# One transfer for q and k of a head, the projection loaded into its place, eight constant products in hash attention with a gated feed-forward block

## The chip, the cores and the metric

The kernel runs on one core of a Trainium2 chip. The metric is device time in microseconds (us). Engines are named as the profile names them: PE is the matrix engine (TensorE; PEld is its loading of weights), DVE the vector engine, ACT the scalar engine, POOL GpSimd, SP the engine that here only issues transfers. SP, ACT and POOL each have a queue of their own in which they issue DMAs.

## The reference

Attention over 4 batches x 8 heads, 768 positions of 64 numbers, in which a query sees only the keys in its own hash bucket; the result goes through a feed-forward block of 3072 tokens x 512, with 2048 inner columns.

```python
q_bits = (np.einsum('bhsd,dk->bhsk', q, proj) > 0).astype(np.int64)
k_bits = (np.einsum('bhsd,dk->bhsk', k, proj) > 0).astype(np.int64)
powers = 2 ** np.arange(n_bits)
q_bucket = np.sum(q_bits * powers, axis=-1)
k_bucket = np.sum(k_bits * powers, axis=-1)
mask = q_bucket[:, :, :, None] == k_bucket[:, :, None, :]
scores = np.where(mask, scale * np.matmul(q, k.transpose(0, 1, 3, 2)), -1000000000.0)
...
attn = attn / (np.sum(attn, axis=-1, keepdims=True) + 1e-09)
...
h = x @ w_in
sp = np.maximum(h, 0.0) + np.log1p(np.exp(-np.abs(h)))
g = h * erf(sp)
return (g @ w_out).astype(np.float32)
```

There are six bits, so `proj` is 64 x 6. q, k, v and `proj` are float32.

## The kernel before

The host transposes q and k and puts them below one another: `qkT` has, for each of 32 heads, 128 rows, 64 of q and 64 of k, of 768 positions each. `proj2` is 128 x 12: `proj` in the upper left and again in the lower right corner, zeros elsewhere. `bucket` is the column 0 to 63, twice.

Attention works on 16 pairs of heads. A pair's q is a tile of 128 partitions (head a in the first 64, head b in the other 64) by 768, k likewise; v has a tile of the same size. They come from a pool in which each of the three names has three buffers (lines 356 to 360 of `fetch`). A pair takes four kinds of work on PE: the hash products (`bits`), the scores (`st`, in float32, plus products of the bits in bf16 that add a large number where buckets agree), the weighted sum of v (`av`), and a product with ones for the divisors (`z`). ACT takes signs of the bits (L400 for pair 0, L865 later) and exponentials (L595). DVE spreads the sign bits (L411, L421) and adds up the exponentials. Later pairs' bits are put in place with DMAs from POOL (L885, L894). Meanwhile POOL loads the weights of the feed-forward block, which ACT and DVE convert. The feed-forward block follows, with PE lines L1256 and L1374.

The beginning is written out by hand. Pair 0 is loaded in halves of 384 positions (`quick`): q of both heads from SP, k of both heads from ACT's queue for the first half, then the second half from SP, eight transfers in all. Meanwhile PE runs `WARM` = 10 products of a tile of ones (L817) whose result nobody reads. Then, for each half, come the hash products (L387), which need the half's q and k and the tile `proj_sb`, and ACT's sign and DVE's spreading; between the halves stand two sets of scores (`plain`). `proj_sb` is 128 x 64: zeros, but for the projection of head a in rows 0 to 63, columns 0 to 5, and that of head b in rows 64 to 127, columns 32 to 37. To build it, POOL loads `proj2` into `proj_in` (L256), DVE clears `proj_sb` (L257) and copies the two blocks (L260). DVE makes a second, narrower arrangement, `proj_q` (L292), for pairs 1 and on. POOL's second transfer brings `row` (L265); from it DVE makes the constants `steps`, `weight` and `weight_q` (L279 to L298).

The order of all else in attention is set by the planner `arrange`: every step is given an engine, a cost, a rank and what it must follow, and the planner lists them. `start_pair` (L808), which calls `fetch` and `fetch_v` for a pair, is a step of SP with a given cost, and is the same step whatever transfers it holds. For pair 1 and on, q and k are four transfers of 64 x 768, and v is two. ACT's `measure` (L671) reads each q and k once more, for a bound on the scores.

In the last pair, the exponentials of the last two blocks of keys (`NS - 2` and `NS - 1`) go into tiles of the load pool, which has nothing more to load: `block` (L580) takes a q, a k and a v tile for each of the two.

Of the kernel before, what the change touches and what calls it, by code (L numbers as in the profile page):

```python
# [54 lines left out]
F32 = mybir.dt.float32  # L55
# [8 lines left out]
P = 128  # L64
# [133 lines left out]
def kernel(  # L198
# [11 lines left out]
    nc = tc.nc  # L210
    B, H, S, D = v.shape
    NBIT = proj2.shape[1] // 2
# [3 lines left out]
    NC = S // P  # L216
# [13 lines left out]
    const = ctx.enter_context(tc.tile_pool(name="const", bufs=1))  # L230
# [2 lines left out]
    small = ctx.enter_context(tc.tile_pool(name="small", bufs=3))  # L233
    QR = 32
    QB = QR // 2
    WARM = 10
    proj_sb = const.tile([P, 2 * QR], F32, name="proj_sb")
    weight = const.tile([P, 2], F32, name="weight")
    proj_q = const.tile([P, QR], F32, name="proj_q")
# [12 lines left out]
    blocks = []  # L252
    stats = const.tile([P, 2, NPAIR, 2], F32, name="stats")
    nc.vector.memset(ones, 1.0)
    proj_in = const.tile([P, 2 * NBIT], F32, name="proj_in")
    nc.gpsimd.dma_start(out=proj_in, in_=proj2)  # L256
    nc.vector.memset(proj_sb, 0.0)  # L257
    for ab in range(2):
        rows = slice(ab * D, ab * D + D)
        nc.vector.tensor_copy(  # L260
            out=proj_sb[rows, ab * QR : ab * QR + NBIT],
            in_=proj_in[rows, ab * NBIT : (ab + 1) * NBIT],
        )
    row = const.tile([P, 1], F32, name="row")
    nc.gpsimd.dma_start(out=row, in_=bucket)  # L265
    steps = const.tile([P, 8], F32, name="steps")
    for c, (end, factor) in enumerate(
# [12 lines left out]
            out=steps[:, c : c + 1],  # L280
# [9 lines left out]
    for ab in range(2):  # L290
        rows = slice(ab * D, ab * D + D)
        nc.vector.tensor_copy(  # L292
            out=proj_q[rows, ab * QB : ab * QB + NBIT],
            in_=proj_in[rows, ab * NBIT : (ab + 1) * NBIT],
        )
    nc.vector.reduce_sum(out=weight_q, in_=steps[:, 5:8], axis=AX.X)
    nc.vector.tensor_tensor(out=weight_q, in0=weight_q, in1=weight[:, 0:1], op=ALU.add)
# [8 lines left out]
    def bank(name):  # L306
        if "X" in kept:
            return kept["X"]
        return misc.tile([P, 512], F32, name=name, tag="bank")
# [43 lines left out]


    def fetch(i, load, quick=False, early=False, into=None):
        d = into or dict(
            q=load.tile([P, S], F32, name="q", tag="q"),
            k=load.tile([P, S], F32, name="k", tag="k"),
            v=load.tile([P, NC, P], F32, name="v", tag="v"),
        )  # L360
        parts = ((0, "q"), (0, "k"), (1, "k"), (1, "q")) if quick else ((None, "q"), (None, "k"))
        for half, what in parts:
            cols = slice(0, S) if half is None else slice(half * HS, half * HS + HS)
            queue = nc.scalar if quick and what == "k" and half == 0 else nc.sync
            for ab in range(2):
                queue.dma_start(
                    out=d[what][ab * D : ab * D + D, cols],
                    in_=qkT[2 * i + ab, "qk".index(what) * D : "qk".index(what) * D + D, cols],
                )
        if not quick and not early:  # L370
            fetch_v(i, d)
        return d

    def fetch_v(i, d):
        b, j = divmod(i, JP)
        for ab in range(2):
            nc.sync.dma_start(
                out=d["v"][:, :, ab * D : ab * D + D],
                in_=v[b, 2 * j + ab].rearrange("(c p) d -> p c d", p=P),
            )  # L380
# [49 lines left out]
    def attention():  # L430
        NS = NPAIR * 4
        with (
# [21 lines left out]
            e_last = {}  # L454
# [125 lines left out]
            def block(n, c):  # L580
                if n == NS - 2 or n == NS - 1:
                    what, m = "qkv"[c], n - (NS - 2)
                    if (m, c) not in e_last:
                        shape = [P, NC, P] if what == "v" else [P, S]
                        room = load.tile(shape, F32, name=what, tag=what)
                        if what == "v":
                            room = room.rearrange("p c d -> p (c d)")
                        e_last[m, c] = room[:, 0:S].rearrange("p (a c) -> p a c", a=2)
                    return e_last[m, c]
                return (e_odd if n // 2 % 2 else e_even)[:, n % 2 * GC + c, :, :]  # L590

            def exponential(n, c):
                st = pairs[n // 4].pop(("st", n, c))
                e = block(n, c)
                nc.scalar.activation(  # L595
                    out=e[:, :, 0:HS], in_=st[:, :, 0:HS], func=AF.Exp, scale=scale
                )
# [21 lines left out]
            def sum_keys(i, k):  # L619
                d = pairs[i]  # L620
                s = wide_sums[i % 2]
                d["sum"] = s[:, :, 0, :, :] if i < NPAIR - 1 else last_sums
                what, _ = sum_steps(i)[k]
                if what is None:
                    into, one, two = s[:, :, 0, :, :], s[:, :, 0, :, :], s[:, :, 1, :, :]
                elif i == NPAIR - 1 and what[0]:
                    k = what[1]
                    into = last_sums[:, 1, :, :]
                    one = into if k > 1 else block(NS - 2, 0)
                    two = block(NS - 2 + k // GC, k % GC)  # L630
                else:
                    half, first, count = what
                    e = (e_odd if half else e_even)[:, :, :, 0:HS]
                    into = one = s[:, half, :, :, :]
                    if count == 4:
                        one, two = e[:, 0:2, :, :], e[:, 2:4, :, :]
                    elif count == 2:
                        two = e[:, 4:6, :, :]
                    else:
                        into, one, two = last_sums[:, 0, :, :], s[:, 0, 0, :, :], s[:, 0, 1, :, :]  # L640
                nc.vector.tensor_tensor(out=into, in0=one, in1=two, op=ALU.add)  # L641
# [166 lines left out]
            def start_pair(i):  # L808
                pairs[i] = fetch(i, load, early=i == 1)
                if i == 1:  # L810
                    for n in range(2):
                        fetch_v(n, pairs[n])

            pairs[0] = fetch(0, load, quick=True)
            warm = bank("warm")
            for n in range(WARM):
                nc.tensor.matmul(  # L817
                    out=warm[0:D, 0:P],
# [102 lines left out]
            for what, n in order:  # L921
                free = slots[-3] if len(slots) >= 3 else ()
                if what == "score":
                    i = n // 4
# [57 lines left out]
            for h in range(NH):  # L982
                i = h // 2
# [3 lines left out]
            for i in range(NPAIR):  # L987
                n = 4 * i
# [108 lines left out]
    def general(pools):  # L1097
# [16 lines left out]
        if True:  # L1114
            for i in range(NPAIR):
                fetch(i, None, into=d)
                b, j = divmod(i, JP)
                for half in range(2):
# [758 lines left out]
```

## Time and profile before

| what | us |
|---|---|
| median of 3 runs | 900.72 |
| lowest and highest of them | 900.38, 900.77 |
| the profiled execution | 900.89 |
| its span in the profile | 899.1 |

The span is what the profile's clock covers; the profiled execution's own time is 1.79 us longer. Times in the profile count from the span's start. Of the transfers concerned, in the DMA view: 30 of 192 KB each for q and as many for k, issued from SP; for pair 0, four of 96 KB for q and two for k from SP, and two for k from ACT. A median of 4.0 us passes from issue to landing for the 192 KB ones of q, 4.4 for those of k; the projection's 6 KB took 2.7 us, the 0.5 KB of `row` 3.0 us. In the profile "x19" behind an operation is how many instructions a line stands for; PE carries out a float32 product in two instructions that the profile counts, and a few records can be missing.

### The profile page before, as it was taken

To read this page: it belongs to the slowest core of one execution; us is meant where nothing else is said; L and a number is where in the kernel's file an instruction comes from. 1 tells how busy PE (TensorE), PEld (TensorE's weight loads), DVE (VectorE), ACT (ScalarE), POOL (GpSimd) and SP (SyncE) were. 2 spreads that over 40 slices of the span, in tenths; PEclk is the share of its full clock that TensorE was granted. 3 is DMA by queue.
4 is the path that set the end of the run, shared out by engine and by line. 5 is a ranking of instruction groups with operands and counts; after the bars stand their busy time and mean duration, and the time that the engine had idled before them with its cause. 6 is when DMAs were issued, how large, how long until landed. Compare 5 with 4: busy or idle time off the path is not lost.

```text
span 899.1 us, 12500 instructions
## 1 busy us (share of the span) xinstructions
PE 893.8 (99%) x4888; PEld 664.5 (74%) x4888; DVE 667.4 (74%) x836; ACT 577.5 (64%) x808; POOL 58.2 (6%) x97
## 2 busy tenths in 40 slices
PE   9999999999999999999999999999999999999998
PEld 5544444454544588888888888888888888888886
DVE  5999999999999879996566556656776656655653
ACT  6888888788887668855555455555655555545520
POOL 1111211111110000000000001000100000000000
PEclk9999999999999999999999999999999999999999
DMA  9557665676652321201231014211421123001321
GB/s 227 135 161 190 191 161 142 174 199 191 169 145 61 102 89 65 82 35 71 59 98 57 23 47 106 82 36 47 103 84 36 36 59 94 35 19 49 87 72 49
DMA packets 65203, 86.95 MB, mean 97 GB/s; under 512 B 34430, under 2 KB 47790, under 8 KB 65136
## 3 DMA queue, kind: packets, MB, share of 16 engines
q1 hardware_dynamic: 56464, 63.81, 25.0%
q0 software_dynamic: 8224, 21.80, 8.7%
q8 instruction: 40, 0.66, 0.3%
q10 hardware_dynamic: 448, 0.46, 0.2%
q14 instruction: 27, 0.22, 0.1%
HBM read 64.71 MB, written 17.40 MB: 91 GB/s over the span
## 4 chain that ended last, share of the span: by engine, by line
PE 99%; ACT 0%; DVE 0%; issue 0%
PE M L1374 32%; PE X L1256 29%; PE st L568 17%; PE av L653 14%; PE M L1256 4%; PE bits L856 1%; PE bits L697 1%; PE warm L817 0%; PE X L1374 0%; PE bits L387 0%; PE z_ps L697 0%; PE X L697 0%; ACT e_even L595 0%; ACT both L400 0%; DVE u L1411 0%
## 5 line engine op out<-in xcount | busy, mean ns | idle before, releaser
L1296 DVE SCALAR_TENSOR_TENSOR e<-w,e 128x1024 f32<-128x1024 f32 x144 | 173.7, 1221 | 8.4 <-ACT w L1290 3.3
L1256 PE MATMUL X<-area,w_in_sb 128*128 128x256 f32 x680 | 160.6, 379 | 0.0
L1290 ACT ACTIVATE w<-h,cq 128x1024 f32<-128x1024 f32 x144 | 155.5, 1137 | 0.0
L568 PE MATMUL st<-q,k 64*128 64x384 f32 x768 | 155.2, 483 | 0.0
L1278 DVE TENSOR_TENSOR h<-X,h 128x512 f32<-128x512 f32 x65 | 44.8, 689 | 144.7 <-PE X L1256 144.7
L1256 PEld LDWEIGHTS X<-area,w_in_sb 128*128 128x128 f32 x680 | 129.2, 190 | 17.6
L1374 PE MATMUL M<-w_out_sb,h 128*128 128x256 f32 x576 | 141.5, 379 | 0.0
L1256 PE MATMUL X<-area 128*128 128x256 f32 x520 | 122.8, 379 | 0.0
L1274 ACT COPY h<-X 128x512 f32<-128x512 f32 x85 | 49.4, 581 | 112.7 <-PE X L1256 112.5
L1374 PEld LDWEIGHTS M<-w_out_sb,h 128*128 128x128 f32 x576 | 109.4, 190 | 14.9
L1256 PEld LDWEIGHTS X<-area 128*128 128x128 f32 x520 | 98.8, 190 | 13.4
L1286 ACT ACTIVATE e<-h,cq 128x1024 f32<-128x1024 f32 x48 | 55.0, 1148 | 79.3 <-DVE h L1278 79.1
L1374 PE MATMUL M<-wt,S 128*128 128x256 f32 x384 | 95.3, 379 | 0.0
L568 PEld LDWEIGHTS st<-q,k 64*128 64x128 f32 x768 | 69.3, 187 | 35.0 <-issue 33.7
L641 DVE TENSOR_TENSOR area<-area 128x1536 f32<-128x1536 f32 (+1 forms) x46 | 79.2, 1721 | 6.7 <-ACT area L595 5.4
L1374 PEld LDWEIGHTS M<-wt,S 128*128 128x128 f32 x384 | 73.0, 190 | 9.9
L595 ACT ACTIVATE e_even<-st 128x768 f32<-128x768 f32 x96 | 73.9, 821 | 0.5 <-PE st L568 0.5
L595 ACT ACTIVATE area<-st 128x768 f32<-128x768 f32 x90 | 72.7, 811 | 0.3 <-PE st L568 0.3
L653 PE MATMUL av<-e_even,v 128*64 128x385 f32 x384 | 65.7, 490 | 0.0
L568 PE MATMUL st<-both 64*128 64x384 bf16 x384 | 64.0, 324 | 0.2 <-ACT e_even L595 0.2
L1311 DVE TENSOR_TENSOR h<-h,e 128x1024 f32<-128x1024 f32 x48 | 58.1, 1221 | 4.0 <-ACT e L1307 4.0
L653 PE MATMUL av<-area,v 128*64 128x384 f32 x360 | 60.6, 486 | 0.0
(135 smaller groups left out, 966.8 us busy)
## 6 DMA issues: line engine op xcount, KB each, us to landing
wt<-wt SPq DMA_DIRECT2D x24, 768.0 KB, 4.3
raw<-in_w_out_dram POOLq DMA_DIRECT2D x16, 512.0 KB, 4.0
raw<-in_w_in_dram POOLq DMA_DIRECT2D x14, 512.0 KB, 4.7
v<-in_v_dram SPq DMA_DIRECT2D x32, 192.0 KB, 4.9
q<-in_qkT_dram SPq DMA_DIRECT2D x30, 192.0 KB, 4.0
k<-in_qkT_dram SPq DMA_DIRECT2D x30, 192.0 KB, 4.4
r<-rd SPq DMA_DIRECT2D x30, 192.0 KB, 3.6
xs<-x SPq DMA_DIRECT2D x15, 384.0 KB, 3.2
```

The lines of the kernel that those rows point to most:

```text
L568: nc.tensor.matmul(out=st[:, ab, 0:HS], lhsT=d["k" + src][rows, keys], rhs=d["q" + src][rows, cols], start=(part == 0), stop=(part == 1),)
L595: nc.scalar.activation(out=e[:, :, 0:HS], in_=st[:, :, 0:HS], func=AF.Exp, scale=scale)
L641: nc.vector.tensor_tensor(out=into, in0=one, in1=two, op=ALU.add)
L653: nc.tensor.matmul(out=d["av", half][rows, 0:w], lhsT=d["v"][:, g * GC + c, rows], rhs=e[:, ab, 0:w], start=(g == 0 and c == 0), stop=(g = ...
L1256: nc.tensor.matmul(out=d[where][:, u, :], lhsT=a[:, kc, f : f + P], rhs=b[:, kc, :], start=(first and u == 0 and kc == 0), stop=(last and ...
L1274: nc.scalar.copy(out=quarter(p, q), in_=st[p][where])
L1278: nc.vector.tensor_tensor(out=h, in0=st[p][where], in1=h, op=ALU.add)
L1286: nc.scalar.activation(out=s, in_=unit(p, v), func=AF.Sigmoid, bias=cq[:, n : n + 1])
L1290: nc.scalar.activation(out=q, in_=unit(p, v), func=AF.Sigmoid, scale=GATE_S[j][0], bias=cq[:, j : j + 1])
L1296: nc.vector.scalar_tensor_tensor(out=s, in0=st[p].pop(("q", v, j)), scalar=GATE_S[j][2], in1=s, op0=ALU.add, op1=ALU.mult,)
L1311: nc.vector.tensor_tensor(out=h, in0=h, in1=st[p].pop(("s", v)), op=ALU.mult)
L1374: nc.tensor.matmul(out=banks["last" if apart and sub else name][:, sub, :], lhsT=a[:, u, sub * P : (sub + 1) * P], rhs=b[:, u, :], start=( ...
```

## The change

Three things, which don't depend on each other.

- q and k of a pair share a tile `qk` of 128 x 2 x 768, three buffers of it as before of each. One transfer brings q and k of a head: 64 partitions, two rows of 768 in each (of 384 for pair 0's halves). A pair takes two transfers of q and k instead of four; pair 0 takes four instead of eight, one of them (the first half of head b) from ACT's queue. Where `fetch` is given tiles from outside (`into`, in the other arm of the kernel, which doesn't run with these inputs), q and k still come apart. The last pair's `block` takes one `qk` tile where it took a q and a k tile.
- The projection is loaded into `proj_sb` at once, behind the clearing of that tile: two blocks of six columns in each of 128 partitions, the zeros of `proj2` among them. `proj_in` and the two copies to `proj_sb` are gone; `proj_q` is copied from `proj_sb`.
- `WARM` is 8.

In the built program the order of instructions on every engine stays, but for these places: on POOL `row` is now loaded ahead of the projection; on DVE the constants from `row` come first, and the two copies to `proj_q` behind the first two sums. On PE the first hash product, which waited for four transfers and DVE, now waits for two transfers of q and k, the projection's transfer, and DVE.

```diff
-    WARM = 10
+    WARM = 8
...
-    proj_in = const.tile([P, 2 * NBIT], F32, name="proj_in")
-    nc.gpsimd.dma_start(out=proj_in, in_=proj2)
     nc.vector.memset(proj_sb, 0.0)
-    for ab in range(2):
-        rows = slice(ab * D, ab * D + D)
-        nc.vector.tensor_copy(
-            out=proj_sb[rows, ab * QR : ab * QR + NBIT],
-            in_=proj_in[rows, ab * NBIT : (ab + 1) * NBIT],
-        )
+    nc.gpsimd.dma_start(
+        out=proj_sb[:, :].rearrange("p (a n) -> p a n", a=2)[:, :, 0:NBIT],
+        in_=proj2.rearrange("p (a n) -> p a n", a=2),
+    )
...
         nc.vector.tensor_copy(
             out=proj_q[rows, ab * QB : ab * QB + NBIT],
-            in_=proj_in[rows, ab * NBIT : (ab + 1) * NBIT],
+            in_=proj_sb[rows, ab * QR : ab * QR + NBIT],
         )
...
     def fetch(i, load, quick=False, early=False, into=None):
-        d = into or dict(
-            q=load.tile([P, S], F32, name="q", tag="q"),
-            k=load.tile([P, S], F32, name="k", tag="k"),
-            v=load.tile([P, NC, P], F32, name="v", tag="v"),
-        )
-        parts = ((0, "q"), (0, "k"), (1, "k"), (1, "q")) if quick else ((None, "q"), (None, "k"))
-        for half, what in parts:
+        d = into
+        if into is None:
+            qk = load.tile([P, 2, S], F32, name="qk", tag="qk")
+            d = dict(q=qk[:, 0, :], k=qk[:, 1, :], v=load.tile([P, NC, P], F32, name="v", tag="v"))
+        for half in range(2) if quick else (None,):
             cols = slice(0, S) if half is None else slice(half * HS, half * HS + HS)
-            queue = nc.scalar if quick and what == "k" and half == 0 else nc.sync
             for ab in range(2):
-                queue.dma_start(
-                    out=d[what][ab * D : ab * D + D, cols],
-                    in_=qkT[2 * i + ab, "qk".index(what) * D : "qk".index(what) * D + D, cols],
-                )
+                rows, head = slice(ab * D, ab * D + D), qkT[2 * i + ab]
+                if into is None:
+                    queue = nc.scalar if half == 0 and ab == 1 else nc.sync
+                    queue.dma_start(
+                        out=qk[rows, :, cols],
+                        in_=head.rearrange("(w r) s -> r w s", w=2)[:, :, cols],
+                    )
+                else:
+                    for n, what in enumerate("qk"):
+                        nc.sync.dma_start(out=d[what][rows, cols], in_=head[n * D : n * D + D, cols])
...
                     if (m, c) not in e_last:
-                        shape = [P, NC, P] if what == "v" else [P, S]
-                        room = load.tile(shape, F32, name=what, tag=what)
                         if what == "v":
-                            room = room.rearrange("p c d -> p (c d)")
-                        e_last[m, c] = room[:, 0:S].rearrange("p (a c) -> p a c", a=2)
+                            room = load.tile([P, NC, P], F32, name="v", tag="v")
+                            rooms = [room.rearrange("p c d -> p (c d)")]
+                        else:
+                            room = load.tile([P, 2, S], F32, name="qk", tag="qk")
+                            rooms = [room[:, k, :] for k in range(2)]
+                        for k, each in enumerate(rooms):
+                            e_last[m, c + k] = each.rearrange("p (a c) -> p a c", a=2)
```

## The prediction

> **What bounds the kernel now.** I read the page's busy shares first, then TensorE's waits, then the chain of waits in order of time, then the timeline of the first ten microseconds, where nearly all that the diff touches happens. The first two settle most of it:
>
> ```profile
> PE 893.8 (99%) x4888; PEld 664.5 (74%) x4888; DVE 667.4 (74%) x836; ACT 577.5 (64%) x808; POOL 58.2 (6%) x97
> ```
>
> ```profile
> PE warm L817 <- DVE ones L254: 1.0, 1, 1.0
> PE st L568 <- ACT e_even L595: 0.2, 1, 0.2
> ```
>
> TensorE is busy 893.8 of 899.1 us and waits for other work twice, 1.2 us in all. So 15 of the 16 loads of a pair, however they are issued, have nothing to gain: no product ever waited for them. What can move is the head, before the products that count begin. The chain (start, length, what) shows it:
>
> ```profile
> 0.99 4.31 PE warm L817 x19
> 5.30 0.97 PE bits L387 x4
> 6.28 1.49 PE st L568 x8
> 7.77 0.84 PE bits L387 x4
> ...
> 8.64 0.58 ACT both L400
> 9.22 0.71 ACT e_even L595
> ...
> 9.97 2.60 PE st L568 x18
> ...
> 26.99 9.95 PE st L568 x72
> ...
> 103.73 9.79 PE st L568 x72
> ...
> 340.42 1.73 PE X L1256 x8
> ```
>
> To be seen: the ten constant products fill TensorE from 0.99 to 5.30 us, and the first hash products follow without a gap, so there they, and no transfer, are what ends last. From 9.97 us on TensorE never stops. The timeline shows when the hash products' operands were there:
>
> ```profile
> 0.74 1.48 SPq L366 DMA_DIRECT2D q<-in_qkT_dram  x2
> 0.75 1.20 ACTq L366 DMA_DIRECT2D k<-in_qkT_dram  x2
> 1.30 0.70 POOL L256 DMA_DIRECT2D proj_in<-in_proj_dram  x1 [0.85 <-POOLq L1857]
> 1.99 0.56 POOL L265 DMA_DIRECT2D row<-in_bucket_dram  x1
> 2.27 1.25 SPq L366 DMA_DIRECT2D k<-in_qkT_dram  x2
> 4.10 0.35 DVE L260 COPY proj_sb<-proj_in 64x6 f32<-64x6 f32 x2 [2.12 <-DMA proj_in<-in_proj_dram]
> 5.02 0.58 DVE L279 TENSOR_SCALAR steps<-row 128x1 f32<-128x1 f32 x8 [0.20 <-DMA row<-in_bucket_dram]
> 5.06 0.18 PEld L387 LDWEIGHTS bits<-k,proj_sb 128*64 128x64 f32 x1
> 7.70 0.13 PEld L387 LDWEIGHTS bits<-q,proj_sb 128*64 128x64 f32 x1 [0.55 <-issue]
> ```
>
> The projection landed at about 4.0 us (2.7 after its issue, by the DMA view) and was in its place at 4.45; the bucket numbers, second on POOL, landed at 5.0 (3.0 after issue). The halves of q and k land 2.5 to 3.3 us after issue, the last at about 4.5. All were ready some 0.8 us before TensorE was.
>
> [...] The granted clock on the page reads 1.00 throughout and doesn't show it, but durations do: a constant product of 128 columns takes 4.31/20 = 0.216 us a pass, as long as a 256-column pass at 340 us (1.73/8). The weight load of one shape takes 0.18 to 0.23 us around 5.1 us and 0.13 at 7.70. So the constant products run at half rate, and the rate doubles near 5.4 us. [...] v takes 4.9 us to land in the median of the run and 6.1 in the first 20 us, where the engines are fullest. [...] here SP's issue hides behind TensorE.
>
> **Part by part.** Two constant products fewer: 2 x 0.431 = 0.86 us. TensorE is then free at 0.99 + 8 x 0.431 = 4.44. This is the most that the head can gain.
>
> q and k in one transfer: the opening issues of the first half fall from four to two. One transfer on SP (0.82 at 0.74) and one on ACT; both are now 64x2x384. The same shape, r<-rd on SP, costs 0.60 to issue, no more than a 64x384 one (0.60), so an issue is paid by the transfer, not by its rows. 384 KB at the 280 GB/s that the DMA view shows between 2.2 and 2.7 us is 1.4 us; first bytes move at 2.05; the first 192 KB, from both queues, landed at 3.25 (2.5 after issue), so some 0.5 after their last byte: 2.05 + 1.4 + 0.5 = 3.95, or 4.4 if the second half's bytes come between. No later than TensorE is free. SP reaches pair 1 four issues, some 2.5 us, earlier. All later pairs save two issues of 0.55 to 0.6 each on SP: nothing, since SP's own work hides under TensorE; if that cover went, two issues a pair would be 1.2 us. A transfer of a pair now waits for the readers of both q and k; the list of instructions shows the same place behind the measures of ACT, and the same slots for the last pair's exponentials, so no new wait there.
>
> Projection into its place: two DVE copies (0.17 each) leave the path to the hash products; the two copies to proj_q (0.34) follow the landing, but only pair 1 at 12.5 us needs them. In return the order on POOL turns over: the bucket numbers go first, at 1.30, the projection second. DVE's memset ends at 1.0, so it isn't waited for. With the first issue at 0.70, the projection's starts at 2.00, and takes the second place's 3.0 to land: 5.0; with the first place's 2.7, 4.7. It is 256 pieces of 24 bytes instead of 128 of 48; both<-bd, 28 pieces, costs POOL 0.58 as 128 pieces do, so I add nothing for issue. I take 4.85. TensorE then needs 0.05 for the signal and the weight load of 0.2 that before was drawn forward under the constant products: hash products at 5.1 against 5.30, 0.2 us gained. The other 0.66 of the removed products turns into waiting for the projection. Behind this wait stand all of TensorE's products; ACT's sign and DVE's spread follow them at the old distance. DVE is through with its constants at 4.85 + 0.1 + 0.34 + 0.5 = 5.8, before the sign at about 6.7.
>
> The bounds of the unknown landing: at best it is there by 4.44 (-0.86). At worst SP, which now issues 192 KB where it issued 96 in the same time, fills the engines: shares of 0.79, 0.75 and 0.60 in the microseconds from 2 to 5 would become full ones[...]. From v's 6.1 against 4.9 I estimate at most 1.2 to 1.5 us more: +1.3.
>
> Sum against the profiled execution (span 899.1, whole 900.89): -0.2. The median of the runs is 900.72, 0.17 below it; the same -0.2 gives 900.5.
>
> **Rivals.** The full gain: row and projection land together and early, 4.44, -0.86, 899.9. For it: they go out 0.7 apart, copies are gone; against it, 3.0 after an issue at 2.00.
>
> The late projection: the fuller engines cost it 1 us or more, hash products after 5.3, +0.3 to +1.3, typically 901.5. For it, the doubled issue rate; against it, that the bytes are tiny.
>
> Slower, the clock: [...] The chain's head work, 0.97 + 1.49 + 0.84 = 3.3 us, begins at 5.1; [...] A later landing makes the gap wider and this likelier.
>
> Gain in the steady part from fewer transfers: the st stretches of the pairs lie between 9.79 and 9.95; their excess over 9.79, summed, is 0.4 us. With the head's, 900.1; the ceiling of everything, 899.5.
>
> **How the numbers follow.** Likeliest, -0.4 to +0.2 with 900.5 (range 900.2 to 900.9): 0.62. Full gain or steady gain: 0.14. Late projection: 0.12. Clock: 0.12. The range of 899.7 to 902.3 leaves out little of the first three and half of the last. A measurement of this kernel can tell about 0.2% from no change, 1.8 us: below 898.9 no case reaches, 0.03 for what I don't see; above 902.5 the clock with a late landing, 0.08; within, 0.89.
>
> **What would show it.** After, the first hash weight load waits for the projection's DMA from about 4.4 to 4.9, and TensorE's busy time falls by 0.86 while its waits grow by some 0.5. No gap there: the full gain. The load after 5.3: the late projection. Weight loads of 0.2 us still at 7 us: the clock. Any wait of TensorE after 13 us, or st stretches away from 9.8, would mean that I misread the later pairs, and the forecast would be wrong for a reason not in it.

## The result, and the profile after

| | median us | lowest to highest | runs |
|---|---|---|---|
| before | 900.54 | 900.16 to 901.17 | 16 |
| changed | 902.45 | 901.30 to 904.15 | 16 |

The changed kernel is slower: the ratio is 1.002, with an interval of 1.0013 to 1.0026. That is 1.8 us by the ratio, and the middle lies just outside the stated range, which ended at 902.3. Not only the middle moved: the runs now spread over 2.9 us where they spread over 1.0. The profiled execution took 902.30 us, its span 900.5.

The page's busy shares and TensorE's waits of the changed kernel:

```profile
PE 894.0 (99%) x4884; PEld 662.3 (74%) x4884; DVE 667.1 (74%) x834; ACT 577.6 (64%) x808; POOL 58.5 (6%) x97
```

```profile
PE bits L386 <- DMA proj_sb<-in_proj_dram: 1.6, 1, 1.6
PE warm L819 <- DVE ones L254: 1.0, 1, 1.0
```

Two constant products are gone, yet TensorE's busy time is not 0.86 lower but 0.2 higher, and there is a new wait of 1.6 us, for the projection. (The profile lets the last constant product end at 4.67; by their pace of 0.43 they end at 4.44.) The chain of waits in order of time (start, length, what) shows both losses:

```profile
1.99 4.23 DMA proj_sb<-in_proj_dram
...
6.31 1.55 PE bits L386 x4
7.86 2.23 PE st L567 x8
10.09 0.82 PE bits L386 x4
...
10.94 0.58 ACT both L399
11.52 0.71 ACT e_even L597
...
12.27 1.78 PE st L567 x11
```

The hash products start at 6.31, where they started at 5.30: 1.0 us later. And the first three stretches take 1.55 + 2.23 + 0.82 = 4.6 us where the same products took 3.3: another 1.3. The steady part begins at 12.27 instead of 9.97, 2.3 us late. The timeline tells why each of the two happened:

```profile
0.74 3.58 SPq L362 DMA_DIRECT2D qk<-in_qkT_dram  x5
0.75 0.71 ACTq L362 DMA_DIRECT2D qk<-in_qkT_dram  x1
...
1.30 0.71 POOL L261 DMA_DIRECT2D row<-in_bucket_dram  x1 [0.85 <-POOLq L1859]
...
1.99 0.74 POOL L256 DMA_DIRECT2D proj_sb<-in_proj_dram  x1
...
5.41 0.58 DVE L275 TENSOR_SCALAR steps<-row 128x1 f32<-128x1 f32 x8 [3.46 <-DMA row<-in_bucket_dram]
...
6.28 0.33 PEld L386 LDWEIGHTS bits<-qk,proj_sb 128*64 128x64 f32 x4 [2.02 <-DVE steps L275]
...
7.79 0.51 PEld L567 LDWEIGHTS st<-qk 64*128 64x128 f32 x4 [1.18 <-issue]
...
8.59 0.34 PEld L567 LDWEIGHTS st<-qk 64*128 64x128 f32 x2 [0.30 <-issue]
...
9.23 0.24 PEld L567 LDWEIGHTS st<-qk 64*128 64x128 f32 x2 [0.30 <-issue]
```

POOL issued as foreseen, `row` at 1.30 and the projection at 1.99. But `row`, 512 bytes, wasn't there before 5.4, and the projection before 6.2. The DMA view (KB each, us from issue to landing) puts it in two numbers, 4.1 and 4.2, where before they were 3.0 and 2.7:

```profile
row<-in_bucket_dram POOLq DMA_DIRECT2D x1, 0.5 KB, 4.1
proj_sb<-in_proj_dram POOLq DMA_DIRECT2D x1, 6.0 KB, 4.2
```

and in the same view of before:

```profile
proj_in<-in_proj_dram POOLq DMA_DIRECT2D x1, 6.0 KB, 2.7
row<-in_bucket_dram POOLq DMA_DIRECT2D x1, 0.5 KB, 3.0
```

The second loss shows in the score products' weight loads: the first of them start at 7.79, the next pairs at 8.59 and 9.23, 0.80 and 0.64 later; the next products start at 9.61, 0.38 after. So TensorE ran at half rate until about 9.3 us; before, until about 5.4. The windows view (stretch, length, then busy time of PE, PEld, DVE, ACT and POOL, granted clock, share of the DMA engines, GB/s) shows fuller engines in these microseconds of the changed kernel:

```profile
2.00:3.00 1.00, 1.00 (x7) 1.00 (x6) 0.00 (x0) 0.84 (x1) 0.74 (x2) 1.00 0.62 127
3.00:4.00 1.00, 1.00 (x6) 1.00 (x5) 0.00 (x0) 0.00 (x0) 0.00 (x0) 1.00 0.96 305
4.00:5.00 1.00, 0.67 (x4) 0.27 (x2) 0.00 (x0) 0.00 (x0) 0.00 (x0) 1.00 1.09 206
```

From 3 us on the shares are 0.96 and 1.09, where before they were 0.75 and 0.60:

```profile
3.00:4.00 1.00, 1.00 (x6) 1.00 (x5) 0.00 (x0) 0.32 (x1) 0.00 (x0) 1.00 0.75 204
4.00:5.00 1.00, 1.00 (x7) 1.00 (x6) 0.66 (x4) 0.00 (x0) 0.00 (x0) 1.00 0.60 172
```

Of the 2.3 us, attention from there to the first feed-forward product gave back 0.16 (302.66 us against 302.82), the feed-forward part up to the last long run of products took the same in both (569.8), and the last stretch of the span, from there on, was 0.7 shorter (15.8 us against 16.5), 0.4 of it a gap before the last products in the profile of before. That leaves the 1.4 by which the spans differ. Nothing in the diff touches the end, and its 0.7 belongs to the one execution of each: over the thirteen profiles of this study the stretch takes 15.5 to 16.6 us, and 16.5 again in e1, which is the changed kernel but for `WARM`.

### The profile page after: what moved, and what is told of

Same layout as the page of the kernel before. It is cut to its first block, busy times and chain, and to the rows that moved or that the text cites. A ratio compares the mean times of both kernels' runs of the same rounds, so it can differ in the third digit from the quotient of the medians.

```text
span 900.5 us, 12400 instructions
## 1 busy us (share of the span) xinstructions
PE 894.0 (99%) x4884; PEld 662.3 (74%) x4884; DVE 667.1 (74%) x834; ACT 577.6 (64%) x808; POOL 58.5 (6%) x97
## 4 chain that ended last, share of the span: by engine, by line
PE 99%; DMA 0%; DVE 0%; ACT 0%; issue 0%; POOL 0%; DVEq 0%; POOLq 0%
PE M L1376 32%; PE X L1258 29%; PE st L567 17%; PE av L655 14%; PE M L1258 4%; PE bits L858 1%; PE bits L699 1%; DMA proj_sb<-in_proj_dram 0%; PE X L1376 0%; PE bits L386 0%; PE z_ps L699 0%; DVE u L1413 0%; PE X L699 0%; ACT e_even L597 0%; POOL row L261 0%
## 5 line engine op out<-in xcount | busy, mean ns | idle before, releaser
L567 PE MATMUL st<-qk 64*128 64x384 f32 x768 | 155.8, 485 | 0.0
L567 PEld LDWEIGHTS st<-qk 64*128 64x128 f32 x768 | 68.9, 188 | 36.7 <-issue 35.6
```

The costliest lines, as they stand in the source:

```text
L567: nc.tensor.matmul(out=st[:, ab, 0:HS], lhsT=d["k" + src][rows, keys], rhs=d["q" + src][rows, cols], start=(part == 0), stop=(part == 1),)
```

## The experiments

Two theories stood against each other at the outset. A: the projection lands late and the gap that TensorE then has costs a second time, because the products behind it run at half rate for longer. B: eight constant products are too few, by their number. C, something in the later pairs, was carried along. Each kernel was timed beside runs of before; the medians of before in the three groups were 900.60, 900.74 and 900.68. "Start" is the first hash product in the profile, "gap" TensorE's idle time before it, counted from the end of the constant products at their pace of 0.43 us (in e1 and e8, where the rate doubled under the last of them, from their end in the profile). Landing, start and gap are those of the one profiled execution; the times are of all runs.

| kernel | q, k in the opening | projection | constant products | landing after issue | start | gap | median | lowest to highest | ratio to before |
|---|---|---|---|---|---|---|---|---|---|
| before | apart | first, two copies | 10 | 2.7 | 5.3 | 0 | 900.54 | 900.16 to 901.17 | 1 |
| changed | together | second, direct | 8 | 4.2 | 6.3 | 1.9 | 902.45 | 901.30 to 904.15 | 1.0013 to 1.0026 |
| e1 | together | second, direct | 10 | 4.3 | 6.4 | 1.2 | 901.66 | 900.89 to 903.39 | 1.0009 to 1.0024 |
| e8 | together | second, direct | 12 | 4.1 | 6.2 | 0.4 | 901.59 | 901.00 to 902.39 | 1.0001 to 1.0014 |
| e2 | together | second, direct | 14 | 4.3 | 7.0 | 0 | 901.54 | 901.09 to 902.16 | 1.0001 to 1.0018 |
| e3 | apart | first, two copies | 8 | 2.9 | 5.1 | 0.6 | 901.05 | 900.64 to 903.17 | 0.9998 to 1.0015 |
| e4 | together | first, two copies | 10 | 4.2 | 5.9 | 0.6 | 900.93 | 900.46 to 901.87 | 0.9997 to 1.0013 |
| e5 | apart | second, direct | 10 | 3.2 | 5.3 | 0 | 901.02 | 900.62 to 901.42 | 0.9994 to 1.0011 |
| e6 | together | first, direct | 8 | 3.9 | 5.3 | 0.9 | 900.84 | 900.25 to 902.62 | 1.0000 to 1.0017 |
| e7 | together | ACT, direct | 8 | not shown | 5.8 | 1.4 | 902.07 | 900.21 to 904.21 | 1.0006 to 1.0019 |
| e9 | together | first, direct | 10 | 4.1 | 5.5 | 0.2 | 900.68 | 899.94 to 900.98 | 0.9990 to 1.0006 |
| e10 | apart | first, direct | 9 | 3.3 | 5.2 | 0.3 | 900.82 | 900.16 to 901.41 | 0.9993 to 1.0010 |
| e11 | apart, later pairs together | first, direct | 9 | 3.3 | 5.2 | 0.3 | 900.85 | 899.89 to 902.34 | 0.9993 to 1.0009 |

### More constant products in the changed kernel (e1, e2, e8)

```diff
-    WARM = 8
+    WARM = 10
```

> The changed kernel with ten constant products again. Theory A (the projection lands late, at 6.2 us[...]): first hash products still at 6.3, gap 1.0 us instead of 1.8; if a gap of 1.0 is short enough the rate doubles near 5.4 and the time is about 901.5 (1.0 over before), if not it stays near 902.4. Theory B (the count of constant products alone does it, the landing costs nothing): back to 900.5. Theory C (the fuller transfers slow something later): 902.4 with the rate doubled early.

(and 14)

> The changed kernel with fourteen constant products, enough to fill TensorE to about 6.3 us. Theory A: hash products at 6.3 with no gap and at full rate, 901.3 to 901.7, a spread as small as before's. Theory B: 900.5. Theory C: 902.4.

(and 12)

> The changed kernel with twelve constant products, which end at 6.17 us, just as the projection lands. Theory A: hash products at 6.3, 0.7 earlier than with fourteen, no gap: 900.9 to 901.2, narrow spread. Theory B: anything from ten up is the same, 901.6.

The chain of waits of e1, with ten:

```profile
1.99 4.35 DMA proj_sb<-in_proj_dram
...
6.43 0.87 PE bits L386 x4
7.29 1.49 PE st L567 x8
8.78 0.82 PE bits L386 x4
```

The start is as late as in the changed kernel, but in this execution the products run at full rate from the first on (0.87 where the changed kernel needed 1.55, 1.49 for 2.23). The time was 901.66, as A had it, but the runs reach up to 903.39: four of the sixteen lie at 903.0 or above. In this execution the rate had doubled before the gap came: the ten products take 4.26 us in the timeline, 4.53 in those of e4 and e9. The spread suggests that it doubled in time in some executions and not in others. With fourteen:

```profile
0.99 6.02 PE warm L819 x27
7.01 0.75 PE bits L386 x4
7.76 1.49 PE st L567 x8
```

These hash products start 0.7 us later than the changed kernel's, and yet the steady part begins 0.8 us earlier (11.43 against 12.27), the profiled execution is 0.6 us faster (901.69 against 902.30) and the median 0.9, in a narrow spread. A start that is later and a kernel that is faster: no theory of the landing alone gives that. What the fourteen products bring is that TensorE isn't idle. With twelve:

```profile
0.99 4.82 PE warm L819 x24
5.82 0.40 issue
6.22 0.87 PE bits L386 x4
```

The spread is narrow again. The time, 901.59, is 0.4 above the upper end of what A expected, and no better than e2's, though this start is 0.8 us earlier. But the two starts are not the work of the two products alone. e2's 28 passes (the line counts 27 of them) take 6.02 us, 0.215 each, which is half rate to within a few tenths of the end; e8's 24 take 0.20 each, because the rate doubled near 5.3 us, under the last of them. With the doubling at 5.3, e2's products too would have ended near 6.2 (an estimate: 20 passes at 0.215 to 5.3, the other 8 at half of that). When the rate doubles differs between executions (near 4.9 us in e1's profile, 5.3 in e8's, 6.9 in e2's, though TensorE does the same work in all three up to 5.2), so a start in the table stands for one execution, and the medians need not follow it; where the other executions started isn't on record. B, by which ten are enough for the old time, fell: all three are about 1 us above before, which is the late start.

### Eight constant products alone (e3)

```diff
-    WARM = 10
+    WARM = 8
```

> The kernel before with eight constant products and nothing else. Theory A: the projection is in place at 4.45, so the hash products start at about 4.5 with no gap to speak of, the rate doubles near 5.4 as before; of the 0.86 us some 0.3 go to hash products at half rate: 900.0 (0.5 under before). Theory B: eight are too few[...]: 901.5 or more.

Chain of waits:

```profile
1.40 3.54 DMA q<-in_qkT_dram
...
5.07 1.64 PE bits L387 x4
6.71 2.86 PE st L568 x8
9.57 1.29 PE bits L387 x4
```

A's number was wrong, 901.05 for 900.0. The last part of q landed at 4.93, 3.5 us after its issue, where no part of the opening that the profile of before shows took more than 3.3; so there was a gap of 0.6 here too. This profile shows half rate from 5.07 to about 10.2, with 2.86 for scores that take 1.49. It took 903.17; one other run lies near it (902.91), eleven at or below 901.30. So a gap of 0.6 us behind eight constant products went with a late doubling in at least the one execution that was profiled, and leaving out two products bought nothing even in the original. e4, below, has the same gap behind ten products and no such run in thirteen; how much of e3's two slow runs is the gap's and how much that of the shorter filling, these runs don't separate.

### q and k together alone (e4), the projection alone (e5)

e4 is the change without its part on the projection and on `WARM`; e5 is the kernel before with that part on the projection alone:

```diff
-    WARM = 8
+    WARM = 10
...
-    nc.gpsimd.dma_start(
-        out=proj_sb[:, :].rearrange("p (a n) -> p a n", a=2)[:, :, 0:NBIT],
+    proj_in = const.tile([P, 2 * NBIT], F32, name="proj_in")
+    nc.gpsimd.dma_start(out=proj_in, in_=proj2)
...
```

(e4, against the changed kernel; the two copies are back as well)

```diff
-    proj_in = const.tile([P, 2 * NBIT], F32, name="proj_in")
-    nc.gpsimd.dma_start(out=proj_in, in_=proj2)
...
+    nc.gpsimd.dma_start(
+        out=proj_sb[:, :].rearrange("p (a n) -> p a n", a=2)[:, :, 0:NBIT],
...
```

(e5, against the kernel before; the two copies to `proj_sb` are gone)

> Only q and k in one transfer; projection by way of its own tile and two copies and first on POOL, ten constant products. Theory A with the fuller transfers as the cause of the late landing: the projection lands 4.1 us after its issue at 1.30, is in place at 5.85, hash products at 5.9, 0.6 us of gap: 901.1 or more. Theory A with POOL's order as the cause: landing at 4.0 as before, hash products at 5.3, 900.5. Theory C: 902.

> Only the projection straight into its place, so second on POOL behind the bucket numbers; q and k apart, ten constant products. Theory A with the fuller transfers as the cause of the late landing: at the old traffic the projection takes 2.7 to 3.0 us from 2.00, lands at 4.7 to 5.0, hash products at 5.3 with no gap: 900.5 to 900.7. Rival (second place and twice the pieces cost the landing whatever the traffic): lands at 6.2, hash products at 6.3, 901.7 as with ten constant products in the changed kernel.

In e4 the chain of waits runs through the projection and its copies:

```profile
1.30 4.15 DMA proj_in<-in_proj_dram
...
5.55 0.16 DVE proj_sb L260
...
5.95 1.00 PE bits L390 x4
```

Only the transfers of q and k differ from before, and the projection, unchanged and first on POOL, takes 4.15 us where it took 2.7. In e5, where q and k are apart, the second place and twice the pieces cost little; the timeline has it in time for a start at 5.31:

```profile
1.99 0.74 POOL L256 DMA_DIRECT2D proj_sb<-in_proj_dram  x1
...
5.28 0.29 PEld L383 LDWEIGHTS bits<-q,proj_sb 128*64 128x64 f32 x2 [0.17 <-issue]
```

Its landing took 3.2 us:

```profile
proj_sb<-in_proj_dram POOLq DMA_DIRECT2D x1, 6.0 KB, 3.2
```

So most of the late landing comes with the transfers of q and k together, and the place on POOL adds the 0.7 us between two issues. Twice the pieces may add a little where q and k are apart: 3.2 and 3.3 in the three such kernels that load the projection directly (e5, e10, e11), 2.7 and 2.9 in the two that copy it (before, e3). Where they are together there is no such difference (3.9 to 4.3 directly, 4.15 with the copies). Fuller engines are the likely reason: of the DMA view's ten slices of 0.2 us from 3 to 5 us, eight or nine are busy by 90% or more in each of the eight profiles with q and k together, and one to three in each of the five with the opening apart. Whether it is that more bytes are asked for at once, or the form of a transfer with two rows in each partition, no run separates. Either of the two parts alone is too small for these runs to tell from nothing: both intervals hold 1.

### The projection from elsewhere (e6, e7), and the gap nearly closed (e9)

```diff
+    nc.vector.memset(row, 0.0)
     nc.gpsimd.dma_start(out=row, in_=bucket)
```

In e6 this clearing makes both of POOL's transfers wait for DVE, and the projection goes first. e7 instead issues the projection from ACT:

```diff
-    nc.gpsimd.dma_start(
+    nc.scalar.dma_start(
         out=proj_sb[:, :].rearrange("p (a n) -> p a n", a=2)[:, :, 0:NBIT],
```

> The changed kernel with the projection first on POOL and the bucket numbers second (a clearing of row makes both wait for DVE). Theory A: lands 4.15 us after 1.30, at 5.45, hash products at 5.55, gap 1.1 with eight constant products: the start is 0.75 better than the changed kernel's, 901.4 to 901.8, still with a wide spread because of the gap. Rival (order on POOL does all the harm): 900.3.

> The changed kernel with the projection issued from ACT, behind its transfer of q and k, instead of from POOL. Theory A: issued at 1.46, lands with or shortly after q and k, between 4.4 and 5.0, hash products at 4.5 to 5.1, gap 0 to 0.6: 900.0 without a gap that counts, 901.0 with one. Rival (q and k themselves, 384 KB and more behind them, land no earlier than the projection): hash products at 6 or later, 902.

In e6's chain of waits the projection lands at 5.23 and the products run at full rate, though after a gap:

```profile
1.32 3.91 DMA proj_sb<-in_proj_dram
...
5.32 0.87 PE bits L387 x4
6.19 1.49 PE st L568 x8
```

Its thirteen runs fall into two groups: seven from 900.25 to 900.84, one at 901.29, five from 902.20 to 902.62. The expected median belonged to neither. The better group is about as fast as before, the other 2.0 us above it (by the means of the two). e7 started at 5.81 and at half rate (1.55 and 2.86 in the same two rows), 902.07. The profile has no landing for the projection from ACT, and names DVE's `steps` as what released the products, though they don't read it; the projection or q and k came last, and which is open. At any rate, issuing it from ACT did not bring the old time back.

Two groups could come from the gap or from the transfers. e9 is e6 with ten constant products (`WARM = 10`):

> The changed kernel with the projection first on POOL and ten constant products. The gap theory (times of the projection-first kernel fall into two groups, near 900.4 and near 902.4[...]): the constant products now end at 5.3, the projection lands at 5.2, no gap, so one group between 900.2 and 901.2, median 900.5. Rival (the two groups come from the transfers, not from the gap): two groups again, the upper one above 902.

One group remained, 899.94 to 900.98, with a median of 900.68, like before's in the same group of runs. Its profile doubles the rate only after the first hash products (chain of waits):

```profile
0.99 4.53 PE warm L820 x20
5.52 1.53 PE bits L387 x4
7.05 1.49 PE st L568 x8
```

The projection landed at 5.4 in this execution and left a gap of 0.2. The doubling was at about 5.4 us in before, with no gap, and near 7 here; in the late cases it was at 9.3 (changed) or about 10.2 (e3). The transfers are the same in e6 and e9, and the upper group went with the gap: five of thirteen runs, then none of thirteen. No execution of e6's upper group was profiled; that such runs stay at half rate longer is read from e3 and e7, whose profiled executions took 903.17 and 903.1.

### The opening apart, the rest together (e10, e11)

e10 has q and k apart, the projection first and direct, nine constant products; e11 is the same but that q and k of pairs 1 to 15 come in one transfer; against e9:

```diff
-    WARM = 10
+    WARM = 9
...
-        for half in range(2) if quick else (None,):
+        for half, what in ((0, "q"), (0, "k"), (1, "k"), (1, "q")) if quick else ():
+            cols = slice(half * HS, half * HS + HS)
+            queue = nc.scalar if what == "k" and half == 0 else nc.sync
+            for ab in range(2):
+                n = "qk".index(what) * D
+                queue.dma_start(out=d[what][ab * D : ab * D + D, cols], in_=qkT[2 * i + ab, n : n + D, cols])
+        for half in () if quick else (None,):
```

> q and k apart as before, the projection straight into its place and first on POOL, nine constant products. The landing theory: light traffic, the projection lands 2.7 to 3.2 after 1.32, by 4.5; the constant products end at 4.87 and the hash products start by 5.1, gap at most 0.2: 900.3 to 900.6, a little under before, one group. Rival (nine are too few by their number): a group above 902.

> As the one with q and k apart and nine constant products, but q and k of pairs 1 to 15 in one transfer; only pair 0 apart. If the harm of the large transfers is in the opening alone, the same time as that one within 0.2, 900.3 to 900.6. If pair 1's transfers of 384 KB, which follow pair 0's on SP, delay the projection or q and k too, hash products 0.5 or more later: 901 or above.

900.82 and 900.85, start 5.2 in both, landing 3.3 in both: the large transfers of the later pairs do neither good nor harm that these runs can tell, and the harm is in the opening. Both are 0.2 us above what was expected, and one run of e11 is at 902.34; before has one such run too, at 902.24, among the 134 of the three groups, so a single one says nothing. No kernel of the study beats the kernel before.

## Why the prediction was wrong, by its own steps

- That TensorE bounds the kernel and that the later pairs' issues are worth nothing was right: from the start of the steady part to the feed-forward block the two kernels differ by 0.16 us, and the medians of e10 and e11 by 0.03.
- "Two constant products fewer: 0.86 us": they were removed and the place became a wait, as the prediction said of most of it; in the end of all of it, and more.
- The order on POOL and the issue at 2.00 were right (1.99). The issue took 0.74 and not 0.56: small. That "an issue is paid by the transfer, not by its rows" held on SP (0.60 again) and not quite on ACT, where the doubled transfer took 0.72 and the single ones 0.56 to 0.61.
- **The step that failed is "I take 4.85"**, the landing of the projection. It took the 2.7 to 3.0 us of the opening before (DMA shares of 0.75 and 0.60 from 3 to 5 us), though the next paragraph noted that SP would issue 192 KB for 96 in the same time. It landed at 6.22: the term is 4.2 us, not 2.85. e4 shows that the transfers of q and k together do most of it (4.15 for the unchanged transfer of the projection), e5 that the place and the pieces by themselves leave it at 3.2. The outer bound, another 1.2 to 1.5, did hold it. The reading to make was the one of fuller engines as the likely case, with `row` and the projection at v's ratio (6.1 to 4.9) or worse. For q and k themselves 3.95 to 4.4 was foreseen; no profile with q and k together shows their landing, but in e6 the hash products, which need them, started at 5.32, so they were there by then.
- **The second failure is in the cases.** "The late projection" and "the clock" stood as rivals with 0.12 each, joined by one sentence ("A later landing makes the gap wider and this likelier") and by the 0.08 left for "the clock with a late landing" above 902.5. They are one chain: a later landing widens the gap (0.6 us in e3, 1.9 in the changed kernel), and behind it the rate doubled only at 9.3 to 10.2 us in the profiles of the changed kernel, e3 and e7. The changed kernel's profile has both, 1.0 for the late start and 1.3 for the half rate. The prediction gave the sum a small chance and priced neither case with it, and its range ended at 902.3. e2 separates them: with no gap, 0.9 us is gone, though the start is later.
- The prediction's upper end, 902.3, was the author's figure for the clock with a start at 5.1; it rested on a time of the doubling that no trace had shown. After a start at 6.31 the half rate cost 1.3 in the changed kernel's profile, and 2.0 lie between e6's groups, with a start of 5.32 in the one profile. The profiles show when the doubling came: with TensorE busy without a gap from 0.99 us on, near 4.9 us (e1), 5.4 (before) or 6.9 (e2), that is 3.9 to 5.9 us after the first product; in the changed kernel, e3 and e7 at 9.3 to 10.2; and the same program, e6, falls into two groups 2.0 us apart. Eight constant products fill 3.45 us, less than the 3.9 of the earliest of these doublings. With a gap behind them the rate had doubled by 5.32 in e6's profile, after a gap of 0.9, and in the changed kernel's not until 9.3. What sets the moment, no run shows. The granted clock reads 1.00 in every microsecond from 1 to 7 us of before, at half rate and at full alike, and can't be used for it.
- Against a late landing the prediction held "that the bytes are tiny". In the changed kernel 6 KB and 0.5 KB wait alike, 4.2 and 4.1 us. How the engines divide their time among the queues, the runs don't show.

## What to carry to other kernels

A small transfer that the first product needs can pay for the large ones issued beside it: here 6 KB took 4.2 us instead of 2.7 once the large ones went out twice as fast, so cutting SP's issue time, which was hidden, cost what wasn't. Filler products ahead of the real ones are not to be counted but to be timed: they must last until the operands are there, in the slowest execution, because an idle TensorE behind them went with a doubling near 10.2 us, where before's came near 5.4, in the profiles of e3 and e7, and with runs 1.3 to 2.1 us above the median (0.6 us idle behind eight products: two runs of thirteen; 0.9 behind eight: five of thirteen; 1.2 behind ten: four of sixteen). And if runs of one program spread into two groups, look for the same products at two speeds in the profile before looking at averages.

## What the runs showed that was not expected

A later start can be faster: in the profiles e2's hash products start 0.7 us after the changed kernel's, and its median is 0.9 us less. Filling alone doesn't set the moment of the doubling: e2's products ran from 0.99 us without a gap and were at half rate until about 6.9, where before's doubled near 5.4. And a queue of its own doesn't make a small transfer early: issued from POOL in first or second place, 6 KB took 3.9 to 4.3 us in every profile with q and k together that shows its landing (seven of them), and 2.7 to 3.3 in all five with the opening apart.
